# Carrying a running phase by a one-row DMA, and filling TensorE's early gaps with dummy matmuls, in a fused linear-attention and MoE kernel

## The chip, the cores and the metric

One core of a Trainium2 chip. The metric is the device time of one execution in microseconds (us).

## The reference

Gated linear attention over 4 sequences, 8 heads, 768 steps and head size 48, followed by a gated MLP on its output (3072 tokens, 384 to 1536 to 384):

```python
for t in range(S):                       # state S_re + i S_im, one per batch and head
    new_re = ar * S_re - ai * S_im       # a_t is complex, its magnitude capped at 0.999
    new_im = ar * S_im + ai * S_re
    S_re, S_im = new_re + kv_t, new_im   # kv_t = outer(k_t, v_t)
    y_t = q_t @ S_re
x = y.transpose(0, 2, 1, 3).reshape(B * S, H * D)
out = (sigmoid(x @ w_gate) * (x @ w_val)) @ w_out
```

## The kernel before

The kernel cuts each sequence into 6 slabs of 128 steps, 24 slabs in all, and takes them in 10 groups. Within a slab the recurrence becomes matmuls; two things pass from slab to slab: the phase (the running sum of the angles of `a`) and the decay (a row of 384 numbers, 8 heads by 48, made by ACT into row 127 of the tile `ee`). All instructions are issued in an order fixed by a table of planned step times.

The phase of a slab (`ct`), in turns, is a triangular matmul over its own angles, plus, for every slab but a sequence's first, a matmul with a constant matrix of ones over `run`. GpSimd (POOL) keeps `run`, the sum of the angle tiles so far. Then the whole turns are taken off (`r16` on DVE, `nid` on TensorE) and ACT takes sine and cosine (`cs`):

```python
nc.tensor.matmul(ct, wt_t, T[A][:, 1, s], start=True, ...)
if prev:
    nc.tensor.matmul(ct, on_t, T[prev[0]], start=False, ...)       # the ones-matmul
# ... POOL: RUN = prev + angles of this slab                        (a copy for the first)
# ... DVE:  r16 = round(ct);  PE: ct -= r16;  ACT: cs = cos, sin
```

`qst` and `kst` are products on DVE of the queries and keys with `cs`; TensorE transposes them (`tp`), DVE copies them out (`qkT`), TensorE multiplies them (`sc`), DVE masks (`mst`).

The decay row goes through HBM so that it comes back as a column on other partitions:

```python
nc.sync.dma_start(scr[b][c:c + 1], T[EE][L - 1:L, 0])               # store: one piece of 1.5 KB
for p0 in (0, 64):                                                  # read: 384 pieces of 4 bytes
    nc.sync.dma_start(rbe[b][p0:p0 + D, lo:hi],                     # a slab, into SBUF, twice
                      scr[b][lo:hi].rearrange("c (h d) -> d c h", d=D))
```

SyncE (SP) issues these and all loads of inputs and stores of results from one queue, in order. The MLP's weights come by POOL's queue. The MLP's matmuls (`g`, `v`, `o`) fill TensorE between the attention's steps. So a slab's chain is load, logarithms and exponentials on ACT, `lm` and `qk` products on POOL, `ct`, `cs`, then DVE and TensorE in turn.

## Time and profile before

| | before |
|---|---|
| median time | 300.29 us (299.94 to 301.54) |
| span of the profiled run, clock | 300.8 us, 0.977 |
| DMA packets | 152,030 |
| TensorE: matmul instructions | 2,328 |

### The profile page before, as it was taken

The page shows a single profiled execution, that of the slowest core. Times are in us where ns is not written, and L with a number is a line of the kernel's source. Part 1 is how long each engine was busy: PE and PEld are TensorE (multiplying, and loading weights), DVE is VectorE, ACT ScalarE, POOL GpSimd, SP SyncE. Part 2 cuts the span into 40 slices and gives each one's busy share as a digit, 9 for nine tenths or more (in the row PEclk, how much of TensorE's full clock was granted, in tenths as well). Part 3 has the DMA queues.
Part 4 walks back from the last instruction along what each step waited for, and adds up shares of the span by engine and source line. Part 5 has one row for each costly group of instructions (what it writes and reads, how often), then busy time and mean ns, then how long its engine had stood idle before and what let it go on. Part 6 is the DMA issues. An engine that isn't in the chain of part 4 may idle for free.

```text
span 300.8 us, 6265 instructions
## 1 busy us (share of the span) xinstructions
PE 258.9 (86%) x2328; PEld 177.2 (59%) x2328; DVE 212.2 (71%) x389; ACT 208.9 (69%) x368; POOL 161.9 (54%) x173
## 2 busy tenths in 40 slices
PE   0443668649999998998999999999999999999995
PEld 0131446436675675866766666566667666766683
DVE  3251268978993699879889976994699889825340
ACT  3663777838978988978996798579668963334341
POOL 0327684966466894898579579727733642100000
PEclk9999987978999999999999999999999999999999
DMA  7999999996793999829392795743820011001011
GB/s 147 171 180 148 183 127 205 128 181 121 147 176 56 158 181 163 143 20 218 55 188 42 129 187 118 135 71 75 142 49 2 26 3 56 1 28 52 26 54 52
DMA packets 152030, 32.69 MB, mean 109 GB/s; under 512 B 144552, under 2 KB 152000, under 8 KB 152000
## 3 DMA queue, kind: packets, MB, share of 16 engines
q1 hardware_dynamic: 148016, 28.76, 54.5%
q0 software_dynamic: 3984, 3.54, 8.3%
q8 instruction: 18, 0.29, 0.4%
q14 instruction: 12, 0.10, 0.1%
HBM read 31.07 MB, written 4.76 MB: 119 GB/s over the span
## 4 chain that ended last, share of the span: by engine, by line
PE 38%; DVE 15%; POOL 14%; issue 10%; ACT 7%; SPq 7%; DMA 7%; DVEq 0%; POOLq 0%; ACTq 0%
PE o L862 10%; PE v L832 8%; PE g L832 8%; SPq L473 4%; POOL lm L514 4%; POOL lm L522 4%; PE cl L556 4%; DVE arr L743 3%; DVE p L848 3%; POOL qk L606 2%; DMA rbe<-scr 2%; DMA a<-in_a_re_dram 2%; DVE mst L729 2%; PE sc L722 2%; DVE kst L676 2%
## 5 line engine op out<-in xcount | busy, mean ns | idle before, releaser
L842 ACT ACTIVATE g<-g 128x384 f16<-128x384 f32 (+2 forms) x120 | 49.1, 427 | 39.1 <-PE g L832 36.9
L848 DVE SCALAR_TENSOR_TENSOR p<-g,v 128x384 f16<-128x384 f16 (+2 forms) x120 | 54.9, 467 | 26.4 <-ACT g L842 12.3
L832 PE MATMUL g<-xt,wg 128*128 128x384 f16 (+2 forms) x360 | 67.7, 298 | 5.0 <-ACT g L842 4.4
L832 PE MATMUL v<-xt,wv 128*128 128x384 f16 (+2 forms) x360 | 67.8, 298 | 0.3 <-DVE p L848 0.2
L862 PE MATMUL o<-wo,p 128*128 128x384 f16 x288 | 56.5, 328 | 0.0
L832 PEld LDWEIGHTS <-wg 128*128 128x128 f16 x360 | 32.3, 99 | 20.4 <-issue 10.0
L606 POOL TENSOR_TENSOR qk<-qk,ee 128x768 f32<-128x768 f32 x23 | 42.3, 1846 | 3.6 <-ACT ee L564 3.3
L832 PEld LDWEIGHTS <-wv 128*128 128x128 f16 x360 | 32.8, 100 | 15.8 <-issue 4.7
L550 POOL TENSOR_TENSOR a<-a 128x384 f32<-128x384 f32 x23 | 25.8, 1143 | 30.2 <-ACT a L540 25.1
L714 DVE COPY qkT<-tp 128x1024 f16<-128x1024 f16 x48 | 32.4, 685 | 12.1 <-PE tp L706 12.0
L514 POOL TENSOR_TENSOR lm<-sq 128x384 f32<-128x384 f32 x23 | 24.9, 1094 | 25.6 <-ACT sq L506 25.3
L887 ACT ACT_TABLE_LOAD x29 | 37.2, 1283 | 0.5
L862 PEld LDWEIGHTS <-p 128*128 128x128 f16 x288 | 27.4, 98 | 16.7 <-issue 1.7
L729 DVE TENSOR_TENSOR mst<-sc,msk_t 128x512 f16<-128x512 f32 x48 | 32.2, 683 | 5.9 <-PE sc L722 5.8
L556 PE MATMUL cl<-lm,wl_t 128*128 128x384 f32 x48 | 22.9, 588 | 11.6 <-ACT lm L535 11.1
L705 PE MATMUL tp<-idn_t,kst 128*128 128x128 f16 x192 | 28.8, 229 | 2.5 <-DVE kst L676 2.5
L676 DVE TENSOR_TENSOR kst<-qk,cs 128x768 f16<-128x768 f32 x24 | 26.8, 1117 | 4.9 <-ACT cs L668 2.9
L706 PE MATMUL tp<-idn_t,qst 128*128 128x128 f16 x192 | 28.3, 229 | 1.6 <-DVE qst L676 1.4
L624 PE MATMUL ct<-a,wt_t 128*128 128x384 f32 x48 | 20.9, 517 | 3.7 <-ACT a L612 3.7
L676 DVE TENSOR_TENSOR qst<-qk,cs 128x768 f16<-128x768 f32 x24 | 23.9, 997 | 0.0
L705 PEld LDWEIGHTS <-kst 128*128 128x128 f16 x192 | 19.7, 103 | 6.7 <-DVE kst L676 4.3
L706 PEld LDWEIGHTS <-qst 128*128 128x128 f16 x192 | 19.6, 103 | 5.6 <-DVE qst L676 2.7
(55 smaller groups left out, 432.7 us busy)
## 6 DMA issues: line engine op xcount, KB each, us to landing
a<-in_a_re_dram SPq DMA_DIRECT2D x24, 192.0 KB
a<-in_a_im_dram SPq DMA_DIRECT2D x24, 192.0 KB
qk<-in_k_dram SPq DMA_DIRECT2D x24, 192.0 KB
qk<-in_q_dram SPq DMA_DIRECT2D x24, 192.0 KB
v<-in_v_dram SPq DMA_DIRECT2D x24, 192.0 KB
out_dram<-ot SPq DMA_DIRECT2D x24, 192.0 KB
wg<-in_moe_w_gate_dram POOLq DMA_DIRECT2D x3, 384.0 KB, 7.0
wv<-in_moe_w_val_dram POOLq DMA_DIRECT2D x3, 384.0 KB, 5.5
```

The lines of the kernel that those rows point to most:

```text
L514: eng(g).tensor_tensor(out=T[LM][:, s], in0=T[SQ][:, 0, s], in1=T[SQ][:, 1, s], op=ALU.add)
L556: nc.tensor.matmul(T[CL][:, :HD], wl_t, T[LM][:, s], start=True, stop=True)
L606: eng(g).tensor_tensor(out=T[QK], in0=T[QK], in1=T[EE], op=ALU.mult)
L676: nc.vector.tensor_tensor(out=T[SL][i].rearrange("p h (r x) -> p h r x", r=2)[:, :, :, 0:D], in0=heads(T[QK][:, i]).unsqueeze(2) .broadcas ...
L705: nc.tensor.transpose(tp[:, 4 + i], ks[:, h], idn_t)
L706: nc.tensor.transpose(tp[:, i], qs[:, h], idn_t)
L729: nc.vector.tensor_tensor(out=T[MS], in0=T[SC], in1=msk_t.unsqueeze(1).broadcast_to([L, 4, L]), op=ALU.mult)
L832: nc.tensor.matmul(T[ACC][:, :nt], w[:, j, fb * 128:fb * 128 + 128], T[XT][:, j, :nt], start=(j == 0), stop=(j == 2))
L842: nc.scalar.activation(out=T[G16][:, :nt], in_=T[PG][:, :nt], func=FT.Tanh, scale=0.5)
L848: nc.vector.scalar_tensor_tensor(out=T[PT][:, fb, :nt], in0=T[G16][:, :nt], scalar=1.0, op0=ALU.add, in1=T[PV][:, :nt], op1=ALU.mult)
L862: nc.tensor.matmul(T[PO][:, :DM], T[PT][:, fb, s * L:(s + 1) * L], wo16[:, fb], start=(fb == 0), stop=(fb == NFB - 1))
L887: nc.scalar.preload_act_table_set(SETS[key[1]])
```

## The change

The intent: TensorE is the bound from 80 us on, so take the ones-matmul off it. For three of the four sequences ACT copies the last row of `ct` (which already is the phase at the slab's end, less its whole turns) out of PSUM, a DMA from POOL's queue moves it from partition 127 to partition 0, and DVE adds it to the first row of the next slab's angles; the triangular matmul then carries it to all rows. In the first third, where TensorE has gaps, 415 dummy matmuls on a tile of zeros hold its clock up. The step times are planned anew. The diff also changes the form of the decay's store and read. Its core (the tables of times, about 440 lines, are cut):

```diff
+ROLL = 1
+WARM = [
+    (0.703, 0, 57), (8.121, 0, 40), (11.569, 0, 11), (12.546, 0, 52),   # time, psum, count
+    ...                                                                 # 21 batches
+]
@@ the decay's row
-                nc.sync.dma_start(scr[b][c:c + 1], T[EE][L - 1:L, 0])
+                with nc.allow_non_contiguous_dma(reason="row turned by heads"):
+                    nc.sync.dma_start(
+                        scr[b][c].rearrange("(d h) -> h d", h=H).unsqueeze(0),
+                        heads(T[EE][L - 1:L, 0]))
...
-                            scr[b][lo:hi].rearrange("c (h d) -> d c h", d=D))
+                            scr[b][lo:hi].rearrange("c (d h) -> d c h", h=H))
@@ the phase
+            rolled = b >= ROLL
+            if rolled and c:
+                def e(T, A=A, s=s, CD=f"cd_{m - 1}"):
+                    nc.vector.tensor_tensor(
+                        out=T[A][:1, 1, s], in0=T[A][:1, 1, s], in1=T[CD],
+                        op=ALU.add)
+                add(("cy", m), e, after=[("atan", g), ("hop", m - 1)], ...)
...
-            if c < NCH - 1:
+            if c < NCH - 1 and not rolled:
                 RUN = t_run(m)
...
+            if rolled and c < NCH - 1:
+                def e(T, CT=CT, CR=CR):
+                    nc.scalar.activation(
+                        out=T[CR][END], in_=T[CT][END, :HD], func=FT.Copy,
+                        scale=lst_t[END])
+                add(("cr", m), e, after=[("nid", m), ("consts", 1)], ...)
+                def e(T, CR=CR, CD=CD):
+                    nc.gpsimd.dma_start(T[CD], T[CR][L - 1:L])
+                add(("hop", m), e, after=[("cr", m)], new=[CD], use=[CR])
@@ the dummies
+            if key[0] == "warm":
+                for _ in range(n):
+                    nc.tensor.matmul(acc[:, :L], zero, zero, start=True, stop=True)
```

## The prediction

> **What bounds the kernel now.** I read the page first, then a table of busy time by stretch, then the matmul groups, then three short pieces of the timeline. The page says that TensorE is busy 86% of the span, and that its idle time lies at the start:
>
> ```profile
> PE   0443668649999998998999999999999999999995
> PEld 0131446436675675866766666566667666766683
> DVE  3251268978993699879889976994699889825340
> ACT  3663777838978988978996798579668963334341
> POOL 0327684966466894898579579727733642100000
> DMA  7999999996793999829392795743820011001011
> ```
>
> Each digit is 7.5 us. PE reads 3 to 8 in the first ten slices and 9 almost everywhere after. In the table by stretch the columns are the stretch, its length, busy time (and count) of PE, PEld, DVE, ACT and POOL, the clock, the DMA share and GB/s:
>
> ```profile
> 40.00:50.00 10.00, 7.58 (x57) 5.41 (x55) 7.63 (x13) 7.45 (x17) 6.27 (x7) 0.66 1.26 192
> 50.00:60.00 10.00, 7.34 (x105) 5.55 (x103) 9.97 (x17) 8.72 (x16) 8.44 (x8) 1.00 0.97 145
> 60.00:70.00 10.00, 5.77 (x39) 4.21 (x39) 8.34 (x11) 5.19 (x9) 5.11 (x7) 0.66 1.17 193
> ...
> 80.00:250.00 170.00, 164.38 (x1570) 113.78 (x1566) 141.93 (x255) 138.29 (x241) 113.46 (x112) 1.00 0.62 107
> ```
>
> So there are two stages. Up to about 70 us the DMA queues are full (share about 1), TensorE is busy 37 of 70 us (the rows of ten us summed), and work goes step by step through DMA, POOL, ACT, DVE and PE. From 80 us on, PE is busy 164.4 of 170 us: there TensorE's in-order queue is the bound, and a microsecond taken off it is worth up to a microsecond. DVE (142 of 170, 83%), ACT (81%) and POOL (67%) are not far behind.
>
> **What the Trainium skill says, and whether the trace agrees.** (1) "TensorE: Matmul & The Clock Gate", Part 1, says that the array runs at half rate until it has been busy for some 3.4 us and falls back after an idle window, so 128-column matmuls start 107 ns or 56 ns apart. The trace agrees:
>
> ```profile
> 18.46 0.31 PE L706 MATMUL tp<-idn_t,qst 128*128 128x128 f16 x1
> 18.57 0.31 PE L705 MATMUL tp<-idn_t,kst 128*128 128x128 f16 x1
> ...
> 49.77 0.22 PE L705 MATMUL tp<-idn_t,kst 128*128 128x128 f16 x1
> 49.83 0.22 PE L706 MATMUL tp<-idn_t,qst 128*128 128x128 f16 x1
> ```
>
> At 18 us the starts are 0.11 apart, at 50 us 0.06. At 44 to 45 us they are 0.11 apart again, so the clock falls back in the early gaps. The clock column has 1.00 at 10 to 20 us all the same, so the spacing is the thing to read.
>
> (2) "SBUF — State Buffer", Who interferes with whom, says that a VectorE instruction with two SBUF inputs is blocked by a GpSimd instruction that reads SBUF, for all of it, because they share a port. The trace has a fine case, a product of 8 columns that normally takes 0.16 us:
>
> ```profile
> 57.90 4.28 DVE L743 TENSOR_TENSOR arr<-rbe 128x8 f32<-128x8 f32 x1
> ...
> 57.48 1.83 POOL L606 TENSOR_TENSOR qk<-qk,ee 128x768 f32<-128x768 f32 x1
> 59.26 0.99 POOL L640 TENSOR_TENSOR run<-run,a 128x384 f32<-128x384 f32 x1
> 60.21 1.93 POOL L514 TENSOR_TENSOR lm<-sq 128x384 f32<-128x384 f32 x2
> ```
>
> It ends at 62.18, as the POOL chain ends at 62.14. The DMA that it needs was issued at 52.3 and its completions arrived by 55.4, so the wait is not the transfer.
>
> (3) "DMA: Bandwidth & Descriptors", Anatomy of one DMA — SWDGE (gpsimd) path, gives a DMA from the GpSimd queue about 2.0 us of fixed time. No such small one is in this trace. The nearest are the row stores of 1.5 KB from the SP queue: 1.13 us from issue to completion with an empty queue, 2.2 to 3.7 us with loads ahead of them.
>
> **The change part by part.** Three of the four sequences (18 of 24 slabs) carry their running phase by a row, not by a summed tile.
>
> *Removed from TensorE:* the ones-matmul for 5 slabs each of 3 sequences, 15 pairs. One pair's worth is read where PE runs densely:
>
> ```profile
> 242.04 0.81 PE L624 MATMUL ct<-a,wt_t 128*128 128x384 f32 x2
> 242.68 0.81 PE L627 MATMUL ct<-run,on_t 128*128 128x384 f32 x2
> 243.33 0.81 PE L862 MATMUL o<-wo,p 128*128 128x384 f16 x4
> ```
>
> 243.33 - 242.68 = 0.65 us, so 15 x 0.65 = 9.7 us. All 15 lie after 80 us, in the stage that TensorE bounds. *Removed from POOL:* 12 sums and 3 copies of a running tile, 12 x 1.05 + 3 x 0.50 = 14.1 us, all of them readers of SBUF.
>
> *Added on ACT:* 15 scaled copies of 384 columns out of PSUM; a copy of that width takes 0.49 us (the output copies), so 7.3 us. *Added on POOL:* 15 issues; those of 384 KB take 0.8 us each, one row should take less, I say 0.4, so 6 us. *Added on DVE:* 15 sums of 384 columns on one row. DVE's time goes by columns (0.56 us for a sum of 384 in f32), and both inputs are in SBUF, so POOL can block them: the 48 products kst and qst average 1.06 us where unblocked ones take 0.95 or less, so 0.1 to 0.2 us each. 15 x 0.73 = 11 us.
>
> *A chain made longer:* a slab's phase now needs the slab before it to pass ct, rounding, subtraction, ACT copy, DMA and DVE sum. From the trace, ct to the start of rounding is 1.0 us with one pair, rounding 0.55, subtraction with its wait 0.5, copy 0.49, DMA 2 to 2.5, sum 0.7: about 5.5 us. Slabs come every 170/14 = some 12 us, but three of a group used to come 2 to 5 us apart, so two links of each group are near the edge and the order must spread them.
>
> *Sums for 80 to 250 us*, if the stretch shrank by all of the 9.7: PE (164.4 - 9.7)/160.3 = 96.5%, DVE (141.9 + 11)/160.3 = 95%, ACT (138.3 + 7.3)/160.3 = 91%, POOL (113.5 - 14.1 + 6)/160.3 = 66%. In-order queues that fetch work from each other do not all run at 95%. I take about half as kept: 5.0 us.
>
> *Dummy matmuls:* the list has 415, 128 columns each, all in the first third: 415 x 0.056 = 23 us warm, 44 cold, against some 33 us that PE is idle in the first 70. They make the first slabs' real matmuls warm. Cold against warm, one slab has two f32 pairs (1.3 against 0.65 each), 16 transposes (1.7 against 0.9) and smaller ones (about 0.4 less): some 2.5 us for a slab. Yet loads, POOL and DVE set the pace there, so of perhaps five cold slabs I credit 1.5 us in all. Where real work is late, the dummies stand in front of it (batches of 26 to 52 take 1.5 to 2.9 us): minus 1.0.
>
> *Also in the diff, though its title is silent on it:* the row of decays is now stored by 384 pieces of 4 bytes and read back by 32 bytes, where it was stored whole and read in 768 pieces of 4 bytes. The pieces fall from about 769 to 480 a slab; the two legs about balance, and I count 0. The new step order I count as what makes the 5.0 possible, and no more.
>
> Sum: 300.3 - 5.0 - 1.5 + 1.0 = 294.8 us.
>
> **The rivals.** *TensorE's work comes off whole:* 96% busy over 170 us speaks for it, and less POOL reading frees DVE. Then 300.3 - 9.7 - 1.5 = 289. *The hop takes the place of the matmul:* if the row's DMA takes 1 us more than planned, PE stands in order before about 8 tight ct's, and 8 of the 9.7 us are given back: 300 to 302. For it speaks that DMA from POOL waits for POOL's own order and that the loads hold the DMA engines at share 0.62; against it that its queue is not the one in which the loads stand. *DVE becomes the bound:* at 95% with blocked sums, waits for p and mst hold PE: 297 to 299. *The start decides:* one blocked product cost 4.3 us at 58 us. New step times deal these collisions anew, so plus or minus 3 us is luck.
>
> **Range and chances.** The sum sits between the full gain (289) and the hop's loss (301), and the collisions add some 3 us either way: 289.5 to 300.5. The 2% lines are 294.3 and 306.3. The first is half a microsecond below my sum: faster 0.45, within 2% 0.50, slower 0.05.
>
> **What would show it.** Right: the table for 80 to 250 has PE at 93 to 96% over fewer matmuls, DVE above 87%; on_t has 10 instructions left; early transposes start 0.055 us apart; the row's DMA lands in 2 to 2.5 us. Wrong: PE waits before ct for the DVE sum of several us in total (the hop rival); DVE's sums average over 1 us (the port); PE idle before 80 us grows, or real matmuls queue behind dummies; or the end moves by the whole 9.7.

## More of the kernel before

A slower state exists, seen in the records as a lower granted clock.

The views that bound the kernel are read in the prediction. Two more serve as a base for what follows. First, the page's busy times with their shares of the span, then the chain of work that ended last, by engine and by line; last, from the list of SyncE's waits, the one before the read-back of the decay (line waited at, releaser, total us, times, longest us):

```profile
PE 258.9 (86%) x2328; PEld 177.2 (59%) x2328; DVE 212.2 (71%) x389; ACT 208.9 (69%) x368; POOL 161.9 (54%) x173
...
PE 38%; DVE 15%; POOL 14%; issue 10%; ACT 7%; SPq 7%; DMA 7%; DVEq 0%; POOLq 0%; ACTq 0%
PE o L862 10%; PE v L832 8%; PE g L832 8%; SPq L473 4%; POOL lm L514 4%; POOL lm L522 4%; PE cl L556 4%; DVE arr L743 3%; DVE p L848 3%; POOL qk L606 2%; DMA rbe<-scr 2%; DMA a<-in_a_re_dram 2%; DVE mst L729 2%; PE sc L722 2%; DVE kst L676 2%
```

```profile
SPq L578 <- DMA scr<-ee: 3.8, 4, 1.2
```

TensorE is the largest part of the chain (38%), DMA is 7%, and of the read-back of the decay (`rbe<-scr`) 2%. The store `scr<-ee` is not among the chain's lines. SyncE waits 3.8 us in all for the decay's store.

## The result, and the profile after

The changed kernel is right and takes 358.38 us median (354.40 to 361.48, 4 runs; two of them, 354.40 and 355.53, fast), against 300.92 (299.94 to 301.81, 4 runs) beside it. Ratios here are the mean time of one kernel's fast runs over the mean of the other's in the same rounds, so not quite the ratio of the medians: 1.180 (95% interval 1.172 to 1.188). The change made the kernel 18% slower; the range of 289.5 to 300.5 us was missed by far. In fast runs the loss is 355.0 - 300.9 = 54 us; the medians, with two slow runs in them, give 57.5, the figure that some expectations below use. The profiled run is a fast one: span 352.6 us, clock 0.927.

The page after, its busy times and its slices (each digit now 8.8 us), then the chain that ended last:

```profile
PE 286.3 (81%) x2713; PEld 202.3 (57%) x2713; DVE 226.9 (64%) x405; ACT 219.7 (62%) x383; POOL 156.7 (44%) x173
...
PE   7868588868589578876986799599677995899995
...
DVE  3530187854457479966996977487569993865431
...
DMA  7977748596596396139439556992500037000111
...
PE 34%; DMA 32%; ACT 9%; DVE 8%; issue 7%; SPq 7%; POOL 1%; DVEq 0%; ACTq 0%
DMA scr<-ee 14%; PE o L933 8%; PE g L903 7%; PE v L903 7%; DMA a<-in_a_re_dram 6%; SPq L515 5%; DMA rbe<-scr 4%; DMA out_dram<-ot 4%; DMA qk<-in_k_dram 3%; PE cl L599 3%; DVE qst L747 2%; PE ct L679 2%; PE tp L777 2%; ACT ee L605 2%; ACT ee L607 2%
```

Read the chain first, because it names what set the end. DMA has gone from 7% to 32% of it, and its largest line is `scr<-ee`, the store of a single row of 384 numbers, which was not among the lines before. TensorE's row in the slices is no longer full from 80 us on (slice 9): 9s are mixed with 5s to 7s up to the last quarter.

The pieces of that chain in order of time (start, duration, what; the longest ones between 40 and 260 us):

```profile
41.04 9.23 DMA qk<-in_k_dram
...
58.11 10.33 DMA scr<-ee
68.49 5.59 DMA rbe<-scr
...
83.40 11.15 DMA a<-in_a_re_dram
...
174.50 9.26 DMA scr<-ee
184.27 3.37 DMA rbe<-scr
...
244.99 11.46 DMA scr<-ee
256.51 1.72 DMA rbe<-scr
```

The store of 1.5 KB takes 9 to 11 us, and the loads of 192 KB at 41.04 and 83.40, each issued some 1 us after stores of such rows (at 38.9 and 39.7, at 82.0 and 82.7), take 9 and 11. The read-back stands after the store: SyncE and, behind it, DVE wait; first SyncE after, then DVE before and after (the last line is the new sum, waiting for its row):

```profile
SPq L624 <- DMA scr<-ee: 38.8, 8, 9.0
```

```profile
DVE arr L743 <- DMA rbe<-scr: 1.6, 3, 0.7
```

```profile
DVE arr L814 <- DMA rbe<-scr: 20.2, 5, 6.3
DVE a L670 <- DMA cd<-cr: 12.5, 4, 5.1
```

SyncE's 3.8 us of waits for the row's store became 38.8. A ring is one of the channels over which a DMA is split; each reports when its share is done. In the completion records a load of 192 KB has reports from 16 rings, the turned store from 8. The last report on record for such a store comes 8.0 to 11.7 us after the issue, median 10.2 (6 of the 24 lack some reports), where the whole row before took 1.13 to 3.73 us, median 1.5.

The table by stretch has for 80 to 250 us (columns as in the prediction):

```profile
80.00:250.00 170.00, 139.47 (x1263) 94.81 (x1263) 124.10 (x217) 126.75 (x217) 100.33 (x104) 0.93 0.63 112
```

TensorE is busy 139.5 us of 170 where it was 164.4: the stage is no longer TensorE's. Its granted clock fell too, to 0.93 in this stretch.

### The profile page after: what moved, and what is told of

Read it like the earlier page. It is cut to its first block, busy times and chain, and to the rows that moved or that the text cites. A ratio compares the mean times of both kernels' runs of the same rounds, so it can differ in the third digit from the quotient of the medians.

```text
span 352.6 us, 7109 instructions
## 1 busy us (share of the span) xinstructions
PE 286.3 (81%) x2713; PEld 202.3 (57%) x2713; DVE 226.9 (64%) x405; ACT 219.7 (62%) x383; POOL 156.7 (44%) x173
## 4 chain that ended last, share of the span: by engine, by line
PE 34%; DMA 32%; ACT 9%; DVE 8%; issue 7%; SPq 7%; POOL 1%; DVEq 0%; ACTq 0%
DMA scr<-ee 14%; PE o L933 8%; PE g L903 7%; PE v L903 7%; DMA a<-in_a_re_dram 6%; SPq L515 5%; DMA rbe<-scr 4%; DMA out_dram<-ot 4%; DMA qk<-in_k_dram 3%; PE cl L599 3%; DVE qst L747 2%; PE ct L679 2%; PE tp L777 2%; ACT ee L605 2%; ACT ee L607 2%
## 5 line engine op out<-in xcount | busy, mean ns | idle before, releaser
L903 PE MATMUL v<-xt,wv 128*128 128x384 f16 (+2 forms) x360 | 70.7, 308 | 11.8 <-ACT ot L943 7.8
L903 PE MATMUL g<-xt,wg 128*128 128x384 f16 (+2 forms) x360 | 71.3, 310 | 7.7 <-ACT g L913 6.8
L913 ACT ACTIVATE g<-g 128x384 f16<-128x384 f32 (+2 forms) x120 | 48.8, 424 | 39.7 <-PE g L903 37.8
L903 PEld LDWEIGHTS <-wv 128*128 128x128 f16 x360 | 33.9, 102 | 29.8 <-issue 17.4
L903 PEld LDWEIGHTS <-wg 128*128 128x128 f16 x360 | 33.8, 102 | 24.4 <-issue 13.6
L965 PE MATMUL warm<-zero 128*128 128x128 f16 x415 | 32.4, 244 | 8.7 <-ACT g L913 7.6
L549 ACT ACTIVATE sq<-a 128x2304 f32<-128x2304 f32 (+2 forms) x10 | 17.4, 1738 | 30.4 <-DMA a<-in_a_re_dram 9.2
L965 PEld LDWEIGHTS <-zero 128*128 128x128 f16 x415 | 29.8, 112 | 10.3 <-issue 8.8
L593 POOL TENSOR_TENSOR a<-a 128x384 f32<-128x384 f32 x23 | 26.9, 1180 | 17.2 <-ACT a L583 16.8
L679 PE MATMUL ct<-a,wt_t 128*128 128x384 f32 x48 | 22.8, 560 | 14.2 <-issue 11.7
L747 DVE TENSOR_TENSOR qst<-qk,cs 128x768 f16<-128x768 f32 x24 | 29.8, 1245 | 0.0
```

Source lines behind the costliest of these rows:

```text
L679: nc.tensor.matmul(ct, wt_t, T[A][:, 1, s], start=True, stop=False, skip_group_check=True)
L747: nc.vector.tensor_tensor(out=T[SL][i].rearrange("p h (r x) -> p h r x", r=2)[:, :, :, 0:D], in0=heads(T[QK][:, i]).unsqueeze(2) .broadcas ...
L903: nc.tensor.matmul(T[ACC][:, :nt], w[:, j, fb * 128:fb * 128 + 128], T[XT][:, j, :nt], start=(j == 0), stop=(j == 2))
L913: nc.scalar.activation(out=T[G16][:, :nt], in_=T[PG][:, :nt], func=FT.Tanh, scale=0.5)
L965: nc.tensor.matmul(acc[:, :L], zero, zero, start=True, stop=True)
```

## The experiments

All runs were right against the reference except the two marked as wrong. "Before" was run beside each batch and stayed at 300.7 to 301.2 us in the median.

### Which part of the change costs 54 us

**The changed kernel with the decay's row whole again.** Everything else of the change stays.

```diff
-  scr[b][c].rearrange("(d h) -> h d", h=H).unsqueeze(0), heads(T[EE][L - 1:L, 0])
+  scr[b][c:c + 1], T[EE][L - 1:L, 0]
-  scr[b][lo:hi].rearrange("c (d h) -> d c h", h=H)
+  scr[b][lo:hi].rearrange("c (h d) -> d c h", d=D)
```

> The changed kernel with one thing undone: the row of decays is stored whole again (one piece of 1.5 KB) and read back in pieces of 4 bytes. Theory S (the turned store, 384 writes of 4 bytes, which landed 9 to 12 us after its issue where the whole row took 1.1 to 3.7, is the whole loss): 290 to 300 us, the value that the prediction would have had without it. Theory H (the new order with the hop of the running phase stalls TensorE; slow stores are only part of a late schedule): above 330 us. If between 305 and 330, both have a share.

Measured: 307.71 us (306.64 to 308.35), ratio to before 1.022 (1.015 to 1.029). In fast runs, undoing this one part takes away 355.0 - 307.6 = 47 of the 54 us, and 7 stay: the third case. The granted clock is back at 0.994; TensorE's 2,713 matmuls are busy 269.6 us here and 286.3 in the changed kernel, so its lower clock can account for at most 17 of the 47 us. Whether it followed from the gaps or had a share of its own was not tested. The chain is TensorE's again:

```profile
PE 46%; DVE 16%; ACT 10%; POOL 9%; issue 7%; DMA 6%; SPq 5%; ACTq 0%; POOLq 0%; DVEq 0%
PE o L930 11%; PE g L900 9%; PE v L900 8%; PE ct L676 4%; SPq L515 4%; PE cl L599 3%; DVE p L916 3%; DVE qst L744 3%; DMA a<-in_a_im_dram 3%; POOL qk L649 2%; DVE qkT L782 2%; ACT g L910 2%; PE tp L774 2%; PE sc L790 2%; PE tp L773 2%
```

**The kernel before with the turned store and read alone.** The same lines put into before, nothing else.

> The kernel before with one thing added: the turned store and the read of 32 bytes; its order, ones-matmuls and cold clock stay. Theory S: 335 to 370 us, with stores landing 8 to 12 us after issue. Theory H: 298 to 308 us, since the order of before has no hop and its DMA legs balance.

Measured: 386.99 us (386.23 to 389.08), ratio 1.287 (1.279 to 1.296). The turned row alone, its store and its read, costs 86 us in the old order, more than in the new one and above Theory S's range. So the largest part of the loss is the part whose effect the prediction set to 0.

**What is left: the dummies.** The first experiment's kernel with an empty list of dummies.

```diff
-WARM = [(0.703, 0, 57), ...]
+WARM = []
```

> The changed kernel with the whole row stored and the 415 dummy matmuls left out. If the dummies help as credited in the prediction (1.5 gained, 1.0 lost by standing in the way): within 1 us of the run with the whole row and dummies. If the warm clock is worth more: 2 to 4 us slower than it. If the dummies stand in front of late work: 2 to 5 us faster than it.

Measured: 311.92 us (310.72 to 312.12), ratio 1.036 (1.030 to 1.042): without the dummies 4.2 us slower. In this order they are worth having.

**The dummies in the old order.** The kernel before with 14 batches, 320 dummies, at its own gaps; 5 rounds.

> The kernel before in its own order with whole rows, with 14 batches of dummy matmuls (320 in all, 128 columns each) put in front of the steps for which TensorE waited over 0.5 us up to 64 us. In the new order the dummies were worth 4.2 us. If the warm clock is what gains: 296 to 299 us. If in this order loads, POOL and DVE set the pace up to 80 us: within 1 us of before.

Measured: 300.48 us (300.35 to 302.39), ratio 0.999 (0.995 to 1.002). No gain, although the dummies do their work: the first slab's transposes start 0.055 us apart at 16.8 us. That they pay only where the order of the other engines is planned for a quick TensorE is argued: the two runs differ in the dummies' places and number as well.

**What is left: the hop.** The first experiment's kernel with the ones-matmuls and POOL's sums back and without `cr`, `hop` and `cy`; the order and the dummies stay.

```diff
-ROLL = 1
+ROLL = 4
...          # POOL's sums are put back into the table of times, cr, hop and cy taken out
```

> The changed kernel with the whole row stored, and the running phase of all four sequences by ones-matmul and POOL sums again, in the new order of all else. By the prediction's sum (9.7 us off TensorE, about half kept): 4 to 6 us slower than the run with the whole row and the hop. If the hop takes the matmul's place: within 1 us of it, or faster.

Measured: 305.39 us (304.38 to 305.72), ratio 1.014 (1.008 to 1.021). The hop costs 307.71 - 305.39 = 2.3 us instead of gaining 4 to 6; the two kernels' times don't overlap. So the 54 us are some 47 for the turned row, 2.3 for the hop and the remaining 4.5 (305.39 - 300.88) for the new order with its dummies. The table for 80 to 250 us shows the exchange, first without the hop, then with it:

```profile
80.00:250.00 170.00, 161.03 (x1524) 110.74 (x1522) 141.88 (x250) 135.88 (x236) 112.64 (x114) 1.00 0.55 108
```

```profile
80.00:250.00 170.00, 153.09 (x1473) 103.63 (x1472) 150.93 (x261) 142.81 (x246) 109.78 (x113) 1.00 0.55 107
```

In the same 170 us TensorE does 161.0 - 153.1 = 7.9 us less, and DVE, at the same time, 150.9 - 141.9 = 9.1 us more. What came off TensorE stands in the table as idle time: 170 - 153.1 = 16.9 us against 9.0.

### Why the hop does not pay

Three explanations: its latency (a `ct` waits for the row), the idle TensorE (its work was not worth what it was taken to be), or the work it adds to the other engines.

**The hop without anyone waiting for it.** The sum goes into a spare row and `ct` doesn't read it. The result is wrong (relative error 0.11).

```diff
-  out=T[A][:1, 1, s], in0=T[A][:1, 1, s], in1=T[CD]
+  out=T[CD],          in0=T[A][:1, 1, s], in1=T[CD]
```

> The changed kernel with the whole row stored and every hop carried out (ACT copy, DMA, DVE sum), but the sum goes to a spare row, so the phase matmul does not wait for it: the result is wrong on purpose. If the hop costs by its latency, which TensorE waits for in order before the phase matmuls (7.8 us idle there in the trace): 298 to 301 us. If it costs by the work on DVE, ACT and POOL: 305 to 308 us, as with the hop read (307.7).

Measured: 306.85 us (306.74 to 306.99), ratio 1.019 (1.015 to 1.022): 0.9 us less than with it, and the two ranges of times overlap. So the wait for the row is at most 0.9 of the 2.3 us, and the most of the cost is elsewhere. TensorE's waits from 80 to 250 us (line, releaser, total us, times, longest) go to DVE's products instead:

```profile
PE sc L790 <- DVE qkT L782: 3.3, 3, 2.3
PE tp L774 <- DVE qst L744: 3.0, 5, 1.2
```

**The kernel before with the work taken off and nothing put in its place.** 15 ones-matmul pairs and POOL's sums of three sequences are gone. Its output is wrong, which doesn't matter for the time.

```diff
-  if prev:                      nc.tensor.matmul(ct, on_t, ...)
+  if prev and b < 1:            nc.tensor.matmul(ct, on_t, ...)
```

> The kernel before with only what the change takes away: no ones-matmul (15 pairs, 9.7 us of TensorE) and no running sums on POOL for three sequences, and nothing in their place; the result is wrong on purpose. If TensorE's queue bounds the stage from 80 us on, as the prediction has it: 291 to 294 us, a gain of 7 to 10. If other in-order queues take over at once: above 296 us.

Measured: 298.81 us (296.96 to 300.83), ratio 0.994 (0.989 to 1.000). By the ratio, 9.7 us of matmuls removed free 1.7 us (0.0057 x 301; by the interval 0 to 3.4). TensorE's waits in 80 to 250 us, by name, in this run and then in the kernel before:

```profile
PE tp L708 <- DVE qst L678: 2.7, 3, 2.2
PE ct L661 <- DVE r L654: 2.7, 7, 0.9
PE y L794 <- POOL x L758: 1.6, 1, 1.6
PE sc L724 <- DVE qkT L716: 1.2, 3, 0.7
```

```profile
PE tp L706 <- DVE qst L676: 0.4, 1, 0.4
PE ct L659 <- DVE r L652: 0.5, 2, 0.3
PE y L792 <- POOL x L756: 1.0, 1, 1.0
PE sc L722 <- DVE qkT L714: 0.2, 1, 0.2
```

The three waits for DVE grow from 1.1 to 6.6 us: DVE, 83% busy in the same stretch, was close behind and took over as soon as TensorE was quicker. This is the ceiling of the idea in this order: even a hop that costs nothing could have gained some 2 us, 3.4 at most.

**The kernel before with the hop's work added, nothing taken away, nobody reading it.** `cr`, the row's DMA and a one-row sum for the 15 slabs.

> The kernel before with only what the change adds for the hop: 15 scaled row copies on ACT, 15 row DMAs from POOL, 15 one-row sums of two SBUF inputs on DVE, whose result nobody reads; nothing is taken away. By the prediction's reckoning this costs some 5 us of the 9.7: 304 to 307 us. If there is slack for it on DVE and ACT: within 1.5 us of before (301). If it costs all that the ones-matmul costs or more: 309 to 313 us.

Measured: 325.57 us (323.17 to 325.97), ratio 1.079 (1.074 to 1.085): 24 us for 15 copies, 15 issues and 15 sums, more than each theory gave. Its order was not planned for these steps. The trace shows POOL standing 21.5 us, in ten waits, at the row's issue until ACT's copy is there; how much of the 24 us that makes is not shown. This run bounds the harm and is not the price in a planned order. TensorE waits for DVE again:

```profile
PE sc L756 <- DVE qkT L748: 5.7, 6, 2.7
PE ct L669 <- DVE r L662: 3.2, 3, 1.7
```

**The sum on POOL.** The first experiment's kernel with `cy` on the engine that the change had relieved.

```diff
-  nc.vector.tensor_tensor(out=T[A][:1, 1, s], ...)
+  nc.gpsimd.tensor_tensor(out=T[A][:1, 1, s], ...)
```

> The changed kernel with the whole row stored and the one-row sum on POOL in place of DVE (right result). DVE loses 12.5 us of work that was partly blocked by POOL; POOL gains some 15 us and had 60% load. If DVE is what the hop costs: 302 to 305 us (the hop unread had 306.9, no hop 305.4). If POOL's order delays the sum and with it the phase matmuls: 308 us or more.

Measured: 315.68 us (312.49 to 316.04), ratio 1.046 (1.039 to 1.052), 8 us slower than on DVE. POOL has more free time in sum, but its place in POOL's order was planned for DVE. So this run says nothing against DVE as the place where it hurts; it only says that POOL's free time doesn't lie where this order needs it.

### Why a store of 1.5 KB takes 10 us

Here the kernel before serves as the bench: it keeps its own whole-row store and gets a second store of each row into a spare place that nobody reads. Only the form of the second store changes from run to run.

**384 pieces of 4 bytes into HBM, on 8 rings**, as in the change.

```diff
+  nc.sync.dma_start(scr2[b][c].rearrange("(d h) -> h d", h=H).unsqueeze(0),
+                    heads(T[EE][L - 1:L, 0]))
```

> The kernel before, as it is, with one store more for each slab: its row of decays also goes out by 384 pieces of 4 bytes to a place in HBM that nothing reads. Nobody waits for these stores. If the loss comes from SP waiting for the store before the read back and the loads behind it in the program: under 310 us. If the loss comes from the pieces themselves, which keep 8 of the 16 DMA rings busy for some 10 us each so that every load behind them is late: 340 to 390 us, as in the kernel before with the turned store (387).

Measured: 394.27 us (393.63 to 397.36), ratio 1.311 (1.305 to 1.317), the last ring's report 10.6 us after the issue (median of 24). Nobody waits for these bytes and the kernel loses 93 us. So a wait for the packed store is not needed for the loss: the pieces delay what comes behind them. The other store, of the whole row, lands 4.1 us after its issue in the median where it was 1.5; SyncE waits 18.8 us for it (3.8 in the kernel before), and DVE 55.5 us for its read-back (1.6):

```profile
SPq L583 <- DMA scr<-ee: 18.8, 4, 6.7
DVE arr L748 <- DMA rbe<-scr: 55.5, 7, 15.0
```

**The same over 16 rings**, 24 pieces each.

> The same extra store, also of 384 pieces of 4 bytes, but cut so that it is spread over 16 rings with 24 pieces each, not 8 with 48. If a ring takes its pieces one by one at some 0.2 us each: landing 5 to 6 us after issue and a loss of about half of the run with 8 rings. If the pieces are limited together (in HBM): landing still near 10 us and the same loss.

Measured: 374.80 us (369.48 to 375.03), ratio 1.235 (1.226 to 1.244), last report 9.2 us. Twice the rings at half the pieces each changes the landing only from 10.6 to 9.2: the time is not a queue of pieces on each ring.

**The same pieces into SBUF**, a spare tile, 8 rings.

```diff
-  scr2[b][c].rearrange("(d h) -> h d", h=H).unsqueeze(0)
+  spare[b][:, :, c]
```

> The kernel before with one DMA more for each slab, as in the extra store of 384 pieces of 4 bytes on 8 rings, but into a spare tile in SBUF, not into HBM. If every 4-byte piece holds its ring for some 0.2 us: landing near 10 us after issue, time near 390 us. If writing small pieces into HBM is what is slow: landing 2 to 4 us, as the read back of 4-byte pieces into SBUF has it, and 301 to 310 us.

Measured: 312.29 us (311.04 to 313.83), ratio 1.037 (1.032 to 1.042), last report 3.3 us. The same count of pieces costs 11 us there and 93 in HBM. But this run changes two things, the target and the neighbourhood: in the spare tile the pieces lie 24 bytes apart, those of each ring in a partition of their own. The next two runs tell the two apart.

**The same into HBM with the pieces 64 bytes apart, and 512 bytes apart.**

```diff
-  scr2[b][c].rearrange("(d h) -> h d", h=H).unsqueeze(0)
+  scr2[b][c].rearrange("(d h x) -> h d x", h=H, x=16)[:, :, 0].unsqueeze(0)    # x=128 for 512
```

> The kernel before with the extra, unread store of 384 pieces of 4 bytes a slab into HBM, as in the run that cost 31%, but the pieces lie 64 bytes apart instead of 4. Theory S (the pieces are slow because neighbours share a line of HBM): the landing falls from 9 to 11 us to 3 to 5 us and the kernel takes 310 to 330 us. Theory W (any 4-byte write into HBM is slow): landing still 8 us or more, 370 to 400 us.

> The same with the pieces 512 bytes apart. Theory S: landing 3 to 4 us, 308 to 325 us, as into SBUF. Theory W: landing still 8 us or more, 370 to 400 us. If only this one is quick and the run with 64 bytes is not, the shared unit lies between 64 and 512 bytes.

Measured: 64 apart 312.74 us (308.55 to 315.27; two of the four runs slow, the profiled one among them), ratio of fast runs 1.030 (1.023 to 1.037), last report 3.5 us; 512 apart 312.00 us (310.84 to 313.44), ratio 1.036 (1.031 to 1.041), last report 3.6 us. The two are the same: 64 bytes of distance are enough. HBM takes small pieces as quickly as SBUF does once they don't lie side by side. The chain of the run with 512 bytes against that with packed pieces:

```profile
PE 29%; DMA 25%; SPq 14%; ACT 10%; issue 8%; POOL 8%; DVE 6%; DVEq 0%; ACTq 0%; POOLq 0%
```

```profile
PE 46%; POOL 12%; DVE 10%; DMA 10%; ACT 8%; issue 6%; SPq 6%; DVEq 0%; POOLq 0%; ACTq 0%
```

DMA falls from 25 to 10% and SyncE's queue from 14 to 6%.

The packets in the traces, which no view above shows one by one, say where the 10 us are not. Of a store late in each run, when the queue is quiet, the 384 pieces start between 1.3 and 2.7 us after the issue, packed or 512 bytes apart alike (issues at 327.46 and 246.70 us), and none takes more than 9 ns. The 8 reports then come at 5.2 to 10.1 us for the packed store and at 2.8 to 3.0 for the spread one. So the pieces leave at the same pace; what is late is their completion. Loads stand meanwhile: 114 of their packets of 192 bytes take over 1 us in the run with the packed extra store (the longest 6.8 us) and 45 in the changed kernel, but one in the kernel before and none with the whole row.

**Half of the row, packed:** 192 pieces, 24 on each of 8 rings.

> The same as the run that cost 31%, packed at 4 bytes, but only half the row: 192 pieces, 24 on each of 8 rings. If the time goes by the number of pieces (both theories), the landing is 4.5 to 6 us and the kernel takes 330 to 355 us. If a fixed cost of the form sets it, landing stays near 9 us and the time above 375 us.

Measured: 383.72 us (381.98 to 386.52), ratio 1.275 (1.268 to 1.281), last report 10.2 us. Both theories had it go with the count of pieces, and it doesn't: half of the pieces land hardly sooner. The third case came true, a fixed cost of the packed form; what it consists of stays open.

**8 bytes apart, each ring in a stretch of its own.** The trace shows 384 pieces over 16 rings here, not 8: 24 pieces, 192 bytes of address for each ring.

```diff
+  scr2[b][c].rearrange("(h d x) -> h d x", h=H, x=2)[:, :, 0].unsqueeze(0)
```

> The kernel before with the extra store of 384 pieces, 8 bytes apart, but each of the 8 rings writes its own stretch of 384 bytes, so that a line of 64 bytes is written by one ring alone. If lines shared between rings are what is slow, it lands in 3 to 4 us and the kernel takes 308 to 325 us, as with the pieces 64 bytes apart. If neighbouring writes of one ring wait for each other as well, it lands in 8 us or more and takes 360 us or more.

Measured: 342.07 us (340.30 to 345.48), ratio 1.136 (1.125 to 1.147), last report 7.0 us (the profiled run is a slow one). Between the two expectations: against the 16 rings that interleave (1.235) it helps to give each ring its own addresses, but a ring's own neighbours still suffer. This form also halves the pieces per 64 bytes, so how much each of the two does is not told apart.

**The changed kernel with its pieces 64 bytes apart.** The turned store stays; the read-back is of 4-byte pieces, one slab at a time.

> The changed kernel with its turned store of 384 pieces kept, but the pieces 64 bytes apart, and read back one slab at a time by pieces of 4 bytes. If the shared lines are what costs the changed kernel its 57 us, the store lands in about 3 us and the kernel takes 306 to 316 us, near the changed kernel with the row stored whole (307.7). If the turned store costs it in another way (SP's issue, more packets), it stays above 330 us.

Measured: 310.31 us (308.48 to 310.90), ratio 1.032 (1.024 to 1.040), last report 3.7 us. SyncE's waits for the store:

```profile
SPq L625 <- DMA scr<-ee: 4.9, 4, 1.7
```

4.9 us instead of 38.8, and in fast runs 355.0 - 310.0 = 45 of the 54 us are back, with as many pieces as in the change. The read-back had to follow (pieces of 4 bytes instead of 32), so two things differ here; since the extra store, whose read-back is untouched, shows the same cost and the same cure, the distance is the cause in the changed kernel too.

No version that computes the right result beats the kernel before by more than the spread: the best is before with dummies, at 0.999.

## Why the prediction was wrong, point by point

**"The two legs about balance, and I count 0": the step that failed, by 47 us in the new order and 86 in the old.** The prediction counted pieces: 769 a slab before, 480 after. The packets did fall, from 152,030 to 145,889. But a count of pieces weighs a 4-byte read from HBM like a 4-byte write into it, and the trace of before held only the first kind: its read-back of 4-byte pieces landed in 2.1 to 5.2 us, and no 4-byte write into HBM was there to be measured. In the runs it took 10.2 us where the whole row took 1.5. The term should have been marked as unmeasured, with the widest range of all. The Trainium skill bears on it: "DMA: Bandwidth & Descriptors", Specifications, says that below 512 bytes a transfer becomes a read-modify-write. By that, each piece of 4 bytes is such a transfer at any distance, and the runs show that size alone doesn't make it slow: 3.5 us with pieces 64 bytes apart, 10.6 packed. That packed pieces wait for each other's read-modify-write of a shared line would fit; it is argued, not shown.

**"A microsecond taken off it is worth up to a microsecond": failed.** The phrase was read from a busy share of 164.4 in 170 us. With the work removed and nothing added, 9.7 us brought 1.7. The prediction halved the gain because DVE would come to 95%, but took the added sums as the reason. Half of the answer was in its own table without them: DVE at 83% and ACT at 81% were close, and DVE's waits grew by 5.5 us when TensorE lost 9.7. A share near 100% says that an engine is busy; what its removal is worth is told by how long the next engine's chain is, and only a run that removes the work measured it.

**The hop: the sizes were nearly right, the net was not.** Row by row, in the changed kernel with the whole row: the copy on ACT 0.573 us (said 0.49), POOL's issue 0.567 (0.4), the sum 0.831 (0.73; 15 x 0.831 = 12.5 us of DVE for 11 said), the landing 1.7 us in the median (2 to 2.5 said). In the changed kernel itself, with the slow stores in the rings, the landing is 2.8 in the median. The group of the sums in the kernel with the whole row, and two of its neighbours:

```profile
L667 DVE TENSOR_TENSOR a<-a,cd 1x384 f32<-1x384 f32 x15 | 12.5, 831 | 2.9 <-ACT a L655 1.6 <-DMA cd<-cr 1.2
L719 ACT ACTIVATE cr<-ct,lst_t 32x384 f32<-32x384 f32 x15 | 8.6, 573 | 4.7 <-PE ct L711 4.4
L727 POOL DMA_DIRECT2D cd<-cr x15 | 8.5, 567 | 29.9 <-ACT cr L719 22.6 <-DMA qk<-in_q_dram 3.8 <-DVE qkT L782 2.6
```

The sums' median is 0.547 us and their longest 1.67: the mean is made by a few long ones. The trace agrees with the port which DVE shares with POOL, the Trainium skill's point that the prediction took from "SBUF — State Buffer": the seven sums of 0.6 us or more all overlap a POOL instruction with two SBUF inputs and end 0.40 to 0.42 us after it (the longest at 153.92, POOL's `qk` at 153.51). The net of +2.3 us is nearest to the prediction's third rival (DVE becomes the bound); the second (TensorE stands before `ct` for the row) is worth at most the 0.9 us by which the unread hop is quicker. Both are read from waits and tables; no run takes the sums' time off DVE without loading another engine.

**The dummies: +1.5 and -1.0, and worth 4.2 in the new order, 0 in the old.** The mechanism was right. Transposes of the first slab start 0.055 us apart in the changed kernel, where they were 0.11 apart before:

```profile
15.96 0.22 PE L776 MATMUL tp<-idn_t,kst 128*128 128x128 f16 x1
16.01 0.22 PE L777 MATMUL tp<-idn_t,qst 128*128 128x128 f16 x1
16.07 0.22 PE L776 MATMUL tp<-idn_t,kst 128*128 128x128 f16 x1
```

The prediction gave them 0.5 us net because other engines pace the start. In the old order that holds within the noise (0.995 to 1.002). In the new one the rest of the start was moved with them (with the whole row the first MLP matmuls stand at 20.7 us, before at 31.1), and taking the dummies away then costs eight times the reckoned amount.

**The new order: "what makes the 5.0 possible, and no more".** With the hop undone and the row whole, the new order and its dummies are 1.4% slower than the old kernel. Since that order was planned for a kernel that has the hop, these runs can't tell what a plan without it would do.

**What would show it: what came of it.** on_t has its 10 instructions and the early transposes are warm, as said. PE at 93 to 96% in 80 to 250 us did not come: 82% in the changed kernel, 90% with the whole row. DVE above 87% came with the whole row (150.9 of 170, 89%). One reading of the page was off as well, without weight in the sum: TensorE's first ten digits run from 0 to 9, not from 3 to 8. The sum of the ranges had no place for a single DMA of 10 us, so the range was wrong, not only its centre: 5% for "slower by over 2%" was far too little while one changed transfer stood in the diff unmeasured.

## What to carry to other kernels

A small store into HBM is not priced by its bytes or its pieces: 384 pieces of 4 bytes side by side took 10 us to complete and held up loads behind them, and 64 bytes between the pieces brought that to 3.5. Price every changed access pattern from a transfer of the same direction, target and spacing in the trace, and where there is none, say so and widen the range. A 97% busy engine is the bound only until its work is taken off: measure the ceiling by removing the work, wrong result and all, before building what replaces it.

## What the Trainium skill lacked or had wrong

- "DMA: Bandwidth & Descriptors", Specifications, gives 512 bytes as the size below which a transfer is a read-modify-write, without a price. Here 384 packed pieces of 4 bytes into HBM took 10.6 us to land and cost a kernel of 301 us 93 us; at 64 bytes apart 3.5 us and 9 us (0.0303 x 301), and at 512 apart no less (3.6 us, 11 us). Of the distance between small writes the page says nothing.
- The same page, Why small descriptors are slow (HBM only), names a fixed cost for each packet and each descriptor, and says that transfers between SBUFs don't suffer. No fixed cost of a piece accounts for 10.6 us packed against 3.5 spread with the same 384 pieces of 4 bytes, nor for 192 packed pieces taking 10.2 us. From SBUF into SBUF the same 384 pieces still cost 3.3 us to land and 11 us of the kernel.
- The same page, Anatomy of one DMA, SWDGE: the fixed 2.0 us holds as a middle for a row of 1.5 KB moved from POOL's queue within SBUF: medians of 1.6 to 2.6 us in the six runs without packed stores. The page lacks what other traffic adds: 2.8 us with packed stores in the rings, 8.0 at the longest.
- The same page has stalled writes holding up an engine's other queues only for remote DMA between cores (Back-pressure in remote DMA); of small stores into HBM and the loads behind them it says nothing. Here a load of 192 KB behind two such stores took 11 us, where the median of its kind before was 3.9.
- "TensorE: Matmul & The Clock Gate", Part 1, agrees (0.11 against 0.055 us between transposes), but no page says that a warm clock is worth what the other engines' order can use of it: 4.2 us here in one order and 0 in another.
